# First layer's opening blocks in two halves of the features, with a new order of the opening

## The chip, the cores and the metric

The kernel runs on one core of a Trainium2 chip. The metric is the device time of one execution in microseconds (us); lower is better.

## The reference

A linear attention with a complex decay, then two layers of a feed-forward network; x has 3072 tokens of 384 columns.

```python
# attention: 4 batches, 8 heads, 768 steps, head width 48
mag = np.sqrt(a_re * a_re + a_im * a_im)
scale = np.minimum(mag, 0.999) / (mag + 1e-06)
for t in range(S):      # S = S * (a_re + i a_im) * scale + outer(k, v); y = q . Re(S)
    ...
# first layer, 384 -> 2048 -> 384
h = x @ w_in
x = (np.maximum(h, 0.0) + alpha * np.minimum(h, 0.0)) @ w_out
# second layer, 384 -> 2048 -> 384
h = x @ w_in2
out = (h - np.tanh(h)) @ w_out2
```

The weights come as 64-bit numbers.

## The kernel before

**The order.** The program is first recorded as operations, each with an engine, a length, what it reads and writes, and a rank ("want"). `Order.issue` then plays a list schedule: of the operations that could start earliest on an engine it takes the one of lowest rank. What it emits is a fixed order for each engine; the engines go through it in order and wait for each other by semaphores. All DMAs are issued from one queue, SP's, in order too: a DMA that waits holds up those behind it. The numbers at the end of the file (`UNITS`, `W_OFF`, `W_WANT`, `SEQ`, `PE_LO` and others) are ranks and choices that set this order.

**Attention.** The tokens are cut in 24 chunks of 128 and 12 units of two chunks; a batch has six chunks. `unit` loads `a_re` and `a_im`, takes squares, logarithms, exponentials and the angle on ACT and DVE, sums logarithms and angles over the steps with a triangular product on PE (L663), and makes `lc` (sum of logarithms, L669), `f` (reduced angle, L674 and L677) and `cs` (cosine and sine, L688 to L692). The cosine is taken from the magnitude of the angle, which L691 writes over `f`. The last row of `f` goes as `carry` to the next unit by a DMA (L682). `chunk` turns `k` and `q`, transposes them (L782), makes the scores (L792), the outputs (L810, L811) and the state (L822), and sends the result to DRAM (`x0d`, L842).

**Weights.** `weights` brings one of 16 features' groups of 128 (f = 0 to 15, "W0" to "W15"): two loads (L469, L467), an L479 on ACT, four integer steps on DVE (L35, L36, L37, L39), a high part on ACT (L487), and a low part: by DVE (L505), or for the f in `PE_LO` by PE and ACT: two halves of an L496 and an L497 product each, and two L499 copies.

**Layers.** `layer` takes blocks of 384 tokens (three chunks). A block's input is loaded as `xf`, split in a high (L865) and a low part (L868), together `xt`. For each f, `h` is a group of nine products (L882); ACT and DVE make `gg` (L889, L892), its high part `ghi` (L900) and low part `glo` (L902); a group of nine products adds them to three `acc` tiles (L913 in the first layer, L915 in the second). Behind f = 15 the three `acc` are copied and sent to DRAM (`x1d`), where the second layer fetches them. PSUM has two tiles for `h` and three for `acc`. `run` puts the eight blocks of the first layer one behind the other, 16 steps of rank each, and ranks the chunks by the block that needs them:

```python
for j in range(n0):
    self.layer(0, j, KF * j)
```

Block 0 needs chunks 0 to 2, which are units 0 and 1, and all 16 weights in its course; block 1 needs chunks 3 to 5.

Of the kernel before, what the change touches and what calls it, by code (L numbers as in the profile page):

```python
# [9 lines left out]
AF = mybir.ActivationFunctionType  # L10
# [342 lines left out]
class Fast:  # L353
# [167 lines left out]
    def unit(self, u, wants):  # L521
# [158 lines left out]
        if (u + 1) % self.UPB and u + 1 < self.NU:  # L680
            cy = ("carry", u + 1)
            self.D_(w0, 1536, lambda: nc.sync.dma_start(  # L682
                out=self.tile(cy, "carry", [1, HD]), in_=T[K("f", 1)][127:128, :]),
                r=[K("f", 1)], w=[cy], new=[(cy, "carry")])
        for c in range(2):
            f, cs = K("f", c), K("cs", c)
            f3 = lambda f=f: T[f].rearrange("p (h d) -> p h d", h=H)
            A(w0, HD, lambda cs=cs, f3=f3: nc.scalar.activation(  # L688
                out=self.tile(cs, "cs", [128, H, 2, D])[:, :, 1, :], in_=f3(), func=AF.Sin, scale=-TWO_PI),
              r=[f], w=[cs], new=[(cs, "cs")], tab=self.rank(u, "sin"))  # L690
            A(w0, HD, lambda f=f: nc.scalar.activation(out=T[f], in_=T[f], func=AF.Abs), w=[f])  # L691
# [32 lines left out]
    def chunk(self, u, j, w0):  # L724
# [23 lines left out]
        if not last:  # L748
            g = K("g")
            self.D_(w0, 1536, lambda: nc.sync.dma_start(out=self.gd[c:c + 1, :], in_=T[e][127:128, :]),  # L750
                    r=[e], w=[K("gd")])
# [5 lines left out]
            self.D_(w0, 1, gload, r=[K("gd")], w=[g], new=[(g, "g")])  # L757
# [90 lines left out]
    def layer(self, ph, j, step):  # L848
# [5 lines left out]
        for kt in range(KD):  # L854
# [17 lines left out]
        accs = [("acc", ph, j, i) for i in range(3)]  # L872
        for f in range(KF):
# [42 lines left out]
            P(step + f - 0.5, 9 * mm_us(n) if ph == 0 else 3 * n // 128 * mm_us(self.DM), g2, r=[gh, gl] + wp, w=accs,  # L916
              new=[(a, "acc") for a in accs] if f == 0 else ())
        for i in range(3):
            o = ("o", ph, j, i)
# [17 lines left out]
            self.D_(step + KF - 2000, 128 * n * 4, st, rate=300e3, r=[o], w=[("xd", 1, j, i)] if ph == 0 else [])  # L937

    def run(self):
# [26 lines left out]
        for j in range(n0):  # L966
            self.layer(0, j, KF * j)
# [74 lines left out]
SEQ = ['k1', 'r1', 'r0', 'a01', 'a00', 'r3', 'v1', 'q1', 'r5', 'r2', 'q0', 'a11', 'r6', 'a10', 'r4', 'k0', 'a21', 'a20', 'v0']  # L1042
# [4 lines left out]
KV_US = 0.85  # L1047
GENERAL = True
# [30 lines left out]
```

## Time and profile before

| | |
|---|---|
| time, median of 3 runs (lowest, highest) | 1079.32 us (1079.24, 1080.22) |
| the profiled execution: its time, its span | 1079.37 us, 1077.7 us |
| PE busy | 1015.8 us, 94% |
| DVE busy | 688.5 us, 64% |
| ACT busy | 612.3 us, 57% |
| moved by DMA | 73.72 MB |

Engines are PE (matrix products; PEld loads its weights), DVE (vector), ACT (scalar functions), POOL and SP (which issues the DMAs). A line such as L882 is the line of the kernel. "idle <-releaser" gives how long the engine stood before an instruction and what it then waited for. Busy shares are means over the span; the opening, in which attention and weights are made ready, has other limits than the rest.

### The profile page before, as it was taken

How to read it: one execution, taken by the hardware profiler on the slowest of the kernel's cores; microseconds unless marked ns; L12 is line 12 of the kernel's file. 1: busy time of each engine (PE TensorE's matmuls, PEld its weight loads, DVE VectorE, ACT ScalarE, POOL GpSimd, SP SyncE). 2: the span in 40 equal slices, each digit the busy share in tenths (PEclk: the TensorE clock that was granted, in tenths of full speed). 3: DMA queues.
4: the chain of work that ended last, by engine and by line, in shares of the span. 5: the costliest groups of instructions: out<-in, count | busy, mean ns of one | idle time of the engine just before them, and what ended most of it. 6: DMA issues, size and time to landing. Idle time of an engine off the chain costs nothing.

```text
span 1077.7 us, 17769 instructions
## 1 busy us (share of the span) xinstructions
PE 1015.8 (94%) x6872; PEld 975.0 (90%) x6872; DVE 688.5 (64%) x1219; ACT 612.3 (57%) x1226; POOL 2.8 (0%) x11
## 2 busy tenths in 40 slices
PE   1469999999999999999999999999999999999996
PEld 1257999999998999999999999999999999999996
DVE  6999987878478776488687489743333333433332
ACT  6987779857487775588574367443323332433331
POOL 1000000000000000000000000000000000000000
PEclk9699999999999999999999999999999999999998
DMA  9764162333223333131324224110101010100000
GB/s 269 188 159 111 31 168 53 74 75 78 59 49 67 60 75 80 46 68 30 75 55 152 89 96 162 59 44 1 44 1 45 1 45 1 45 8 23 16 8 26
DMA packets 184471, 73.72 MB, mean 68 GB/s; under 512 B 146469, under 2 KB 180281, under 8 KB 184377
## 3 DMA queue, kind: packets, MB, share of 16 engines
q1 hardware_dynamic: 184376, 72.49, 26.1%
q8 instruction: 56, 0.92, 0.4%
q14 instruction: 39, 0.31, 0.1%
HBM read 58.27 MB, written 14.19 MB: 67 GB/s over the span
## 4 chain that ended last, share of the span: by engine, by line
PE 81%; ACT 8%; DVE 5%; issue 2%; DMA 2%; SPq 1%; ACTq 0%; DVEq 0%
PE h L882 32%; PE acc L915 19%; PE acc L913 15%; PE x L782 4%; PE x L792 4%; PE x L810 2%; PE x L822 2%; PE x L811 2%; PE x L663 1%; DMA w<-in_moe_w_in_dram 1%; DVE glo L902 1%; ACT w L487 1%; SPq L543 1%; ACT ghi L900 1%; DVE gg L892 0%
## 5 line engine op out<-in xcount | busy, mean ns | idle before, releaser
L882 PE MATMUL h<-xt,w 128*128 128x384 f32 x2160 | 404.0, 337 | 5.2 <-DVE gg L892 4.1
L882 PEld LDWEIGHTS h<-xt,w 128*128 128x128 f32 x2160 | 375.7, 188 | 9.7 <-DVE gg L892 6.0
L902 DVE TENSOR_TENSOR glo<-gg,ghi 128x384 fp32r<-128x384 f32 x256 | 142.2, 556 | 99.0 <-ACT ghi L900 98.9
L900 ACT CAST ghi<-gg 128x384 fp32r<-128x384 f32 x256 | 131.2, 513 | 125.2 <-PE acc L915 42.6
L913 PE MATMUL acc<-ghi,w 128*128 128x384 f32 x768 | 199.9, 341 | 0.0
L915 PE MATMUL acc<-w,ghi 128*128 128x384 f32 x672 | 171.5, 336 | 1.8 <-ACT ghi L900 1.8
L898 DVE TENSOR_TENSOR gg<-h,gg 128x384 f32<-128x384 f32 x128 | 71.0, 554 | 157.8 <-ACT gg L896 157.8
L896 ACT ACTIVATE gg<-h 128x384 f32<-128x384 f32 x128 | 63.0, 492 | 163.9 <-PE h L882 159.5
L913 PEld LDWEIGHTS acc<-ghi,w 128*128 128x128 f32 x768 | 136.2, 188 | 3.5 <-issue 2.9
L913 PE MATMUL acc<-glo,w 128*128 128x384 f32 x384 | 129.1, 336 | 0.3 <-DVE glo L902 0.2
L915 PEld LDWEIGHTS acc<-w,ghi 128*128 128x128 f32 x672 | 121.9, 189 | 2.1 <-ACT ghi L900 2.1
L915 PE MATMUL acc<-w,glo 128*128 128x384 f32 x336 | 112.9, 336 | 0.0
L892 DVE SCALAR_TENSOR_TENSOR gg<-gg,nal,h 128x384 f32<-128x384 f32 x128 | 78.0, 610 | 47.2 <-ACT gg L889 46.7
L889 ACT ACTIVATE gg<-h 128x384 f32<-128x384 f32 x128 | 62.3, 487 | 56.2 <-PE h L882 54.5
L913 PEld LDWEIGHTS acc<-glo,w 128*128 128x128 f32 x384 | 72.1, 188 | 1.2 <-DVE glo L902 1.2
L915 PEld LDWEIGHTS acc<-w,glo 128*128 128x128 f32 x336 | 63.5, 189 | 0.2 <-DVE glo L902 0.2
L782 PE MATMUL x<-idt,kqt 128*112 128x128 f32 x384 | 55.2, 281 | 6.8 <-ACT w L499 6.4
L782 PEld LDWEIGHTS x<-idt,kqt 128*112 128x112 f32 x384 | 44.2, 137 | 12.4 <-ACT w L499 6.9
L792 PE MATMUL x<-qT,kT 112*128 112x128 f32 x384 | 51.2, 276 | 1.6 <-ACT kT L784 1.5
L792 PEld LDWEIGHTS x<-qT,kT 112*128 112x128 f32 x384 | 49.5, 192 | 3.5 <-ACT kT L784 2.6
L784 ACT COPY qT<-x 112x512 f32<-112x512 f32 x48 | 28.1, 586 | 34.9 <-PE x L782 32.5
L811 PE MATMUL x<-sc,v 128*48 128x128 f32 (+1 forms) x384 | 37.7, 274 | 0.0
(209 smaller groups left out, 1191.6 us busy)
## 6 DMA issues: line engine op xcount, KB each, us to landing
w<-in_moe_w_in_dram SPq DMA_DIRECT2D x16, 384.0 KB
w<-in_moe_w_out_dram SPq DMA_DIRECT2D x16, 384.0 KB
raw<-in_moe_w_in_dram SPq DMA_DIRECT2D x16, 384.0 KB
raw<-in_moe_w_out_dram SPq DMA_DIRECT2D x16, 384.0 KB
q<-in_q_dram SPq DMA_DIRECT2D x24, 192.0 KB
k<-in_k_dram SPq DMA_DIRECT2D x24, 192.0 KB
v<-in_v_dram SPq DMA_DIRECT2D x24, 192.0 KB
x0d<-sc SPq DMA_DIRECT2D x48, 96.0 KB
```

The lines of the kernel that those rows point to most:

```text
L782: nc.tensor.transpose(o[:, i, :], T[t][:, 4 * half + i], self.idt)
L792: nc.tensor.matmul(o[:, i, :], T[kT][:, i, :], T[qT][:, i, :], start=True, stop=True)
L811: nc.tensor.matmul(oh, cols(T[K("v")]), T[sc][:, i, :], start=first, stop=True)
L882: nc.tensor.matmul(o, w[:, a, kt * 128:(kt + 1) * 128], x[:, b_, kt, :n], start=i == 0, stop=i == len(mms) - 1)
L889: A(E, n, lambda h=h, g=g: nc.scalar.activation(out=mt(g, "gg"), in_=T[h][:, :n], func=AF.Relu, scale=-1.0), psum=True, r=[h], w=[g], new= ...
L892: V(E, n, lambda f=f, g=g, h=h: nc.vector.scalar_tensor_tensor(T[g][:, :n], in0=T[g][:, :n], scalar=self.nal[:, f:f + 1], in1=T[h][:, :n], ...
L896: A(E, n, lambda h=h, g=g: nc.scalar.activation(out=mt(g, "gg"), in_=T[h][:, :n], func=AF.Tanh), psum=True, r=[h], w=[g], new=[(g, "gg")], ...
L898: V(E, n, lambda h=h, g=g: nc.vector.tensor_tensor(T[g][:, :n], T[h][:, :n], T[g][:, :n], op=ALU.subtract), psum=True, r=[h], w=[g])
L900: A(E, n, lambda g=g, gh=gh: nc.scalar.copy(mt(gh, "ghi", F32R), T[g][:, :n]), r=[g], w=[gh], new=[(gh, "ghi")])
L902: V(E, n, lambda g=g, gh=gh, gl=gl: nc.vector.tensor_tensor(mt(gl, "glo", F32R), T[g][:, :n], T[gh][:, :n].bitcast(F32), op=ALU.subtract), ...
L913: nc.tensor.matmul(acc[:, :n], w[:, b_, i * 128:(i + 1) * 128], gs[a][:, :n], **kw)
L915: nc.tensor.matmul(acc, gs[a][:, i * 128:(i + 1) * 128], w[:, b_, :], **kw)
```

## The change

Each of blocks 0 and 1 is taken in two pieces of eight features. The order of the pieces is block 0 with f 0 to 7, block 1 with f 0 to 7, block 0 with f 8 to 15, block 1 with f 8 to 15, then blocks 2 to 7 whole. The first piece's sums are copied and sent to `x1d` in DRAM as before; the second piece loads them back into `xf` tiles (`part`), adds them to its `acc` on DVE and stores the result. For units 0 to 2 the magnitude of the angle goes to the place in `a` where the angle was, no longer over `f`. DMAs of `carry` and of the state's factor get a very low rank (`SOON`), so they are issued as soon as the planner has them ready. All ranks are new, and `PE_LO` has nine features, formerly five.

```diff
-            A(w0, HD, lambda f=f: nc.scalar.activation(out=T[f], in_=T[f], func=AF.Abs), w=[f])
...
+            m, key = f, [f]
+            if u < LATE:
+                m, key = ("turn", u, c), [arc[c]]
+            mag = lambda m=m, c=c: T[m] if m[0] == "f" else X("ai")[:, c * HD:(c + 1) * HD]
+            A(w0, HD, lambda f=f, mag=mag: nc.scalar.activation(out=mag(), in_=T[f], func=AF.Abs), r=[f] if u < LATE else [], w=key)
...
-    def layer(self, ph, j, step):
+    def layer(self, ph, j, step, f0=0, f1=None):
...
-        for kt in range(KD):
+        f1 = f1 or KF
+        for kt in range(KD) if f0 == 0 else ():
...
-        for f in range(KF):
+        for f in range(f0, f1):
...
+            if f0:
+                self.D_(done + 2000 - PART_AHEAD, 128 * n * 4, lambda i=i, part=part: nc.sync.dma_start(
+                    out=self.tile(part, "xf", [128, self.NB])[:, :n], in_=self.xd[1][i * 128:(i + 1) * 128, t0:t0 + n]),
+                    rate=300e3, r=[("xd", 1, j, i)], w=[part], new=[(part, "xf")])
...
+            if f0:
+                V(done, n, lambda i=i, o=o, part=part: nc.vector.tensor_tensor(
+                    self.tile(o, "sc", [128, self.NB])[:, :n], T[accs[i]][:, :n], T[part][:, :n], op=ALU.add),
+                  psum=True, r=[accs[i], part], w=[o], new=[(o, "sc")])
...
-            self.D_(w0, 1536, lambda: nc.sync.dma_start(
+            self.D_(w0 - SOON, 1536, lambda: nc.sync.dma_start(
...
-        for j in range(n0):
-            self.layer(0, j, KF * j)
+        for j, f0, f1 in PIECES:
+            self.layer(0, j, begin[j, f0], f0, f1)
...
+PIECES = [(0, 0, 8), (1, 0, 8), (0, 8, 16), (1, 8, 16)] + [(j, 0, 16) for j in range(2, 8)]
...
-PE_LO = (0, 3, 5, 7, 11)
+PE_LO = (1, 2, 3, 4, 5, 6, 8, 10, 11)
```

`UNITS`, `C_WANT`, `AHEAD`, `W_OFF`, `W_WANT`, `LATE_RANK` and `SEQ` get new values. In the changed file lines from 692 on stand 5 to 7 lower (L742 is L747, L882 is L889, L913 is L920). What the ranks do to the order is seen in three places.

SP's queue at the start, before (`w_112`, `w_117` are raw weights of W1 and W0, later ones of W3, W5, W2; `a` is unit 0's):

```order
L469 DMA w_112<-in_moe_w_in_dram 128x3x128
L467 DMA w_112<-in_moe_w_out_dram 128x384
L469 DMA w_117<-in_moe_w_in_dram 128x3x128
L467 DMA w_117<-in_moe_w_out_dram 128x384
L543 DMA a<-in_a_re_dram 128x8x48
L543 DMA a<-in_a_im_dram 128x8x48
```

and now, with the rows around the `carry` transfer further down (`w_123` and `w_132` are W0 and W1; `w_139` and `w_193` are the places of unit 1's and unit 2's `a`):

```order
L543 DMA a<-in_a_re_dram 128x8x48
L543 DMA a<-in_a_im_dram 128x8x48
L543 DMA a<-in_a_re_dram 128x8x48
L543 DMA a<-in_a_im_dram 128x8x48
L469 DMA w_123<-in_moe_w_in_dram 128x3x128
L467 DMA w_123<-in_moe_w_out_dram 128x384
...
L682 DMA carry<-f 1x16x24
L737 DMA q<-in_q_dram 128x8x48
L543 DMA w_139<-in_a_re_dram 128x8x48
L543 DMA w_139<-in_a_im_dram 128x8x48
L543 DMA w_193<-in_a_re_dram 128x8x48
L543 DMA w_193<-in_a_im_dram 128x8x48
```

The four loads of `a` moved ahead of the first weights, and the second halves of the next two units' `a` behind the `carry` of unit 0.

DVE ahead of the first `lc`, before (one piece of eleven rows; weight steps of W0 and W1 lie between the attention's):

```order
L35 TENSOR_SCALAR raw<-raw 128x768
L576 TENSOR_SCALAR hl<-a 128x384
L35 TENSOR_SCALAR raw<-raw 128x768
L36 TENSOR_SCALAR raw<-raw 128x768 x2
L579 SCALAR_TENSOR_TENSOR sq<-sq 128x384
L576 TENSOR_SCALAR hl<-a 128x384
L37 SCALAR_TENSOR_TENSOR raw<-w_112,raw 128x768
L37 SCALAR_TENSOR_TENSOR raw<-w_117,raw 128x768
L579 SCALAR_TENSOR_TENSOR sq<-sq 128x384
L39 SCALAR_TENSOR_TENSOR raw<-w_112,raw 128x768
L39 SCALAR_TENSOR_TENSOR raw<-w_117,raw 128x768
```

and now, where the weight steps begin with the first `lc`:

```order
L576 TENSOR_SCALAR hl<-a 128x384
L579 SCALAR_TENSOR_TENSOR sq<-sq 128x384
L576 TENSOR_SCALAR hl<-a 128x384
L579 SCALAR_TENSOR_TENSOR sq<-sq 128x384
L590 TENSOR_TENSOR hl<-hl,sq 128x384
L599 SCALAR_TENSOR_TENSOR sq<-sq,a 128x384
...
L669 TENSOR_SCALAR lc<-acc 128x384
L35 TENSOR_SCALAR raw<-raw 128x768 x2
L669 TENSOR_SCALAR lc<-acc 128x384
L36 TENSOR_SCALAR raw<-raw 128x768 x2
```

Eight weight steps moved from ahead of the first `lc` to behind it.

PE at the first `h` groups, before (`w0_177` is W0, `acc_987` the first of three sums):

```order
L882 MATMUL h_916<-xt_866,w0_177 128x384 x9
L882 MATMUL h_933<-xt_866,w1_173 128x384 x9
L882 MATMUL h_955<-xt_866,w2_253 128x384 x9
L882 MATMUL h_972<-xt_866,w3_264 128x384 x9
L913 MATMUL acc_987<-ghi_965,w0_177 128x384 x2
L913 MATMUL acc_987<-glo_970,w0_177 128x384
```

and now (`w10_967` is W10, whose low part PE makes):

```order
L889 MATMUL h_915<-xt_870,w0_214 128x384 x9
L889 MATMUL h_932<-xt_870,w1_203 128x384 x9
L889 MATMUL h_954<-xt_870,w2_282 128x384 x9
L920 MATMUL acc_975<-ghi_964,w0_214 128x384 x2
L920 MATMUL acc_975<-glo_969,w0_214 128x384
...
L496 MATMUL x_996<-raw_696,idt_72 128x384
L497 MATMUL x_996<-w10_967,hl_115 128x384
L496 MATMUL x_1004<-raw_696,idt_72 128x384
L497 MATMUL x_1004<-w10_967,hl_115 128x384
```

Three groups stand ahead of the first `acc`, and a pair for W10 stands behind it.

## Rows read from the trace of the kernel before

**Rows 1.** Page, part 1: busy time, share of the span, instructions of each engine.
```profile
PE 1015.8 (94%) x6872; PEld 975.0 (90%) x6872; DVE 688.5 (64%) x1219; ACT 612.3 (57%) x1226; POOL 2.8 (0%) x11
```

**Rows 2.** Stretches: length, busy us (count) of PE, PEld, DVE, ACT, POOL; PEclk, DMA share, GB/s.
```profile
27.00:54.00 27.00, 12.58 (x30) 6.19 (x30) 26.20 (x44) 25.48 (x46) 0.00 (x0) 0.62 0.80 188
54.00:81.00 27.00, 17.77 (x186) 13.91 (x186) 26.66 (x44) 23.18 (x42) 0.00 (x0) 0.94 0.59 157
81.00:108.00 27.00, 24.75 (x225) 19.61 (x223) 26.45 (x43) 20.72 (x42) 0.00 (x0) 0.93 0.45 111
108.00:135.00 27.00, 25.89 (x206) 24.87 (x207) 26.57 (x46) 20.04 (x37) 0.00 (x0) 1.00 0.17 31
...
162.00:189.00 27.00, 26.82 (x153) 25.75 (x151) 20.85 (x39) 25.12 (x54) 0.00 (x0) 1.00 0.24 55
189.00:216.00 27.00, 27.00 (x233) 25.89 (x233) 23.78 (x43) 23.14 (x47) 0.00 (x0) 1.00 0.37 72
```

**Rows 3.** Waits of PE after 110 us: total us, times, longest.
```profile
PE h L882 <- DVE gg L892: 2.5, 3, 1.1
PE acc L915 <- ACT ghi L900: 1.8, 1, 1.8
PE h L882 <- DVE gg L898: 0.8, 1, 0.8
```

**Rows 4.** Stretches between milestones, columns as in Rows 2.
```profile
22.58:104.87 82.29, 54.62 (x430) 38.69 (x428) 80.64 (x134) 70.25 (x132) 0.00 (x0) 0.83 0.63 154
112.34:180.70 68.36, 68.18 (x473) 65.54 (x472) 58.98 (x100) 53.88 (x104) 0.00 (x0) 1.00 0.39 98
```

**Rows 5.** Timeline of ACT: start us, us, engine, line, operation [idle before <-releaser].
```profile
7.94 1.28 ACT L479 ACT_TABLE_LOAD   x1 [7.94 <-DMA w<-in_moe_w_out_dram]
...
10.82 0.51 ACT L567 ACTIVATE sq<-a 128x384 f32<-128x384 f32 x1
```

**Rows 6.** Stretches of two microseconds, columns as in Rows 2.
```profile
2.00:4.00 2.00, 0.00 (x0) 0.00 (x0) 1.34 (x1) 0.00 (x0) 1.87 (x3) 1.00 0.90 273
4.00:6.00 2.00, 0.00 (x0) 0.00 (x0) 0.32 (x1) 0.00 (x0) 0.24 (x3) 1.00 0.99 326
6.00:8.00 2.00, 0.00 (x0) 0.00 (x0) 0.00 (x0) 0.06 (x1) 0.00 (x0) 1.00 1.10 313
8.00:10.00 2.00, 0.00 (x0) 0.00 (x0) 0.00 (x0) 1.99 (x2) 0.00 (x0) 1.00 1.12 215
```

**Rows 7.** Timeline of DVE: first lc, three after it, the third xt.
```profile
22.58 0.55 DVE L669 TENSOR_SCALAR lc<-acc 128x384 f32<-128x384 f32 x1
23.05 0.55 DVE L35 TENSOR_SCALAR w<-w 128x768 f32<-128x768 f32 x1
23.51 0.95 DVE L505 TENSOR_TENSOR w<-raw,w 128x768 fp32r<-128x768 f32 x1
24.38 0.55 DVE L36 TENSOR_SCALAR w<-w 128x768 int32<-128x768 int32 x1
...
104.33 0.54 DVE L868 TENSOR_TENSOR xt<-xf,xt 128x384 fp32r<-128x384 f32 x1
```

**Rows 8.** Timeline of PE: a weight-lo pair of two halves, and what follows it.
```profile
95.38 0.91 PE L496 MATMUL x<-w,idt 128*128 128x384 f32 x2
...
97.13 1.05 PE L792 MATMUL x<-qT,kT 112*128 112x128 f32 x8
```

**Rows 9.** Timeline of PE: first h groups, first acc group.
```profile
103.41 4.04 PE L882 MATMUL h<-xt,w 128*128 128x384 f32 x18
109.11 3.39 PE L882 MATMUL h<-xt,w 128*128 128x384 f32 x18 [1.66 <-DVE gg L892]
112.34 0.51 PE L913 MATMUL acc<-ghi,w 128*128 128x384 f32 x2
```

**Rows 10.** Waits of SP's own queue: total us, times, longest.
```profile
SPq L682 <- DVE f L677: 7.9, 2, 7.7
```

**Rows 11.** Chain of waits, in order of time: start us, us, what.
```profile
63.05 3.30 DMA x0d<-sc
```

More of the change, by code (lines that the diff above doesn't have):

```diff
@@ L871, in layer @@
         subs = [xt + (kt, i) for kt in range(KD) for i in range(2)]
-        accs = [("acc", ph, j, i) for i in range(3)]
-        for f in range(KF):
+        accs = [("acc", ph, j, f0, i) for i in range(3)]
+        for f in range(f0, f1):
             W = ("W", ph, f)
@@ L883, in g1 @@
                                      start=i == 0, stop=i == len(mms) - 1)
-            P(step + f, 9 * mm_us(n), g1, r=[xt] + subs + wp, w=[h], new=[(h, "h")])
+            P(step + f - f0, 9 * mm_us(n), g1, r=[xt] + subs + wp, w=[h], new=[(h, "h")])
             mt = lambda key, tag, dt=F32: self.tile(key, tag, [128, self.NB], dt)[:, :n]
-            E = step + f - 1000
+            E = step + f - f0 - 1000
             if ph == 0:
@@ L908, in g2 @@
                 for i in range(3):
-                    acc = self.tile(accs[i], "acc", [128, self.NB], psum=True) if f == 0 else T[accs[i]]
+                    acc = self.tile(accs[i], "acc", [128, self.NB], psum=True) if f == f0 else T[accs[i]]
                     for jj, (a, b_) in enumerate(((0, 0), (0, 1), (1, 0))):
-                        kw = dict(start=f == 0 and jj == 0, stop=f == KF - 1 and jj == 2)
+                        kw = dict(start=f == f0 and jj == 0, stop=f == f1 - 1 and jj == 2)
                         if ph == 0:
@@ L915, in g2 @@
                             nc.tensor.matmul(acc, gs[a][:, i * 128:(i + 1) * 128], w[:, b_, :], **kw)
-            P(step + f - 0.5, 9 * mm_us(n) if ph == 0 else 3 * n // 128 * mm_us(self.DM), g2, r=[gh, gl] + wp, w=accs,
-              new=[(a, "acc") for a in accs] if f == 0 else ())
+            P(step + f - f0 - 0.5, 9 * mm_us(n) if ph == 0 else 3 * n // 128 * mm_us(self.DM), g2, r=[gh, gl] + wp, w=accs,
+              new=[(a, "acc") for a in accs] if f == f0 else ())
+        done = step + f1 - f0 - 2000
         for i in range(3):
-            o = ("o", ph, j, i)
+            o, part = ("o", ph, j, f0, i), ("part", j, i)
+            if f0:
+                self.D_(done + 2000 - PART_AHEAD, 128 * n * 4, lambda i=i, part=part: nc.sync.dma_start(
+                    out=self.tile(part, "xf", [128, self.NB])[:, :n], in_=self.xd[1][i * 128:(i + 1) * 128, t0:t0 + n]),
+                    rate=300e3, r=[("xd", 1, j, i)], w=[part], new=[(part, "xf")])
             end = ph == 1 and j == len(self.blocks[1]) - 1
@@ L936, in st @@
                     nc.sync.dma_start(out=self.out[t0 + i * 128:t0 + (i + 1) * 128, :], in_=T[o])
-            self.D_(step + KF - 2000, 128 * n * 4, st, rate=300e3, r=[o], w=[("xd", 1, j, i)] if ph == 0 else [])
+            self.D_(done, 128 * n * 4, st, rate=300e3, r=[o], w=[("xd", 1, j, i)] if ph == 0 else [])
     def run(self):
@@ L959, in run @@
                 self.tile(neg, "hl", [128, 128], F32R), self.idt, -1.0, None, op0=ALU.mult), w=[neg], new=[(neg, "hl")])
+        begin, step = {}, 0
+        for j, f0, f1 in PIECES:
+            begin[j, f0] = step
+            step += f1 - f0
         for u in range(self.NU):
-            late = [KF * self.where[2 * u + c][0] - AHEAD + self.where[2 * u + c][1] / 256 + (c and C_WANT) for c in range(2)]
+            late = [begin[self.where[2 * u + c][0], 0] - AHEAD + self.where[2 * u + c][1] / 256 + (c and C_WANT) for c in range(2)]
             self.unit(u, UNITS[u] if u < len(UNITS) else [late[0], late[0], *late])
@@ L965, in run @@
             self.weights(0, f, W_WANT[0] + W_WANT[1] * f + (W_OFF[f]))
-        for j in range(n0):
-            self.layer(0, j, KF * j)
+        for j, f0, f1 in PIECES:
+            self.layer(0, j, begin[j, f0], f0, f1)
         for f in range(KF):
```

32 lines of the change are left out of this document (17 added, 15 removed).

## The prediction, made before the changed kernel was run

> **What bounds the kernel now.** I read the page first, then stretches of 27 us, then the waits of PE, then the three timelines around the first `h` product. The sum is made against the profiled execution, 1079.37 us (span 1077.7 us and 1.7 around it); the median of the three runs, 1079.32 us, is the same number for this purpose. A difference of about 0.2% (2.2 us) is what a measurement of this kernel can tell from none.
>
> The page says that PE is busy in 94% of the span [rows 1]. The reader should see in the stretches where the other 6% lie: PE worked 12.58, 17.77 and 24.75 us of the second to fourth stretch of 27 us, and nearly all of every later one [rows 2]. After 110 us it waited 5.1 us in all, in five waits [rows 3]. So the end is the moment at which PE can work without a break, plus the PE work left then, plus those few waits. Everything that the change can win lies in the first 112 us.
>
> In those, DVE is the limit: from its first `lc` to its third `xt` it was busy for 80.64 of 82.29 us, ACT for 70.25 [rows 4]. The timelines give the milestones: the first Square of the attention on ACT at 10.82 us, behind a table load and two weight steps that waited for weights until 7.94 [rows 5]; the first `lc` on DVE at 22.58; the third `xt` of block 0 at 104.33, the last input of an `h` group [rows 7]; the first `h` at 103.41 (a group's first products need less), with a wait of 1.66 us behind it, and the first `acc` product at 112.34 [rows 9].
>
> **The change, part by part.** Prices are starts of one instruction to starts of the next. On DVE 384 columns take 0.47 us (22.58 to 23.05), L35 and L36 with 768 columns 0.46, other work on 768 columns 0.87 (23.51 to 24.38) [rows 7].
>
> *A. Earlier head.* The four loads of `a_re` and `a_im` now stand first on SP, and ACT begins with a table load and the Square, no longer with weight steps. When do the loads land? Before, four weight loads (1.57 MB) stood first. 273, 326 and 313 GB/s in the slices from 2 to 8 us [rows 6] mean that they were through at about 7.2 us, and ACT started on the second pair at 7.94 [rows 5]: 0.75 us later. The pieces of `a` move more slowly; the slice from 8 to 10 us, in which they ran, has 215 GB/s [rows 6]. 197 KB at that rate are 0.9 us; from 2.3 us on that gives 3.2, with the 0.75 it is 4.0 us, and behind the table load of 1.28 us [rows 5] the Square starts at about 5.3. That is 5.5 us earlier. Ends: 6.2 earlier if the load runs at the full 326 GB/s and lands at once, 2.5 if the second pair holds the chain up. ACT and DVE have the same attention steps from there to the first `lc` as before, and the weight steps between them (5.4 us of DVE) only filled waits; so the whole head moves, and `lc` starts near 17.1.
>
> *B. DVE from the first `lc` to the third `xt`.* I count instructions in the two orders. The attention of chunks 0 to 3 stands ahead of the third `xt` in both. Now in this stretch: one L36, one L37 and two L39 more (0.47 + 0.87 + 1.74), and one L677 (0.47); gone are three L505 (2.61), one L576 and one L579 of the next unit (0.47 + 0.87), and two L614 of 768 columns (1.74). That is 2.1 us less of the 82.3. Its waits were 1.65 us before [rows 4]; I keep them. Ends: 1.7 us less, if nothing waits any more, and 4 more, if ACT now makes DVE wait: ACT has about as much work ahead of the third `xt` as before (three L479 and one L487 fewer; one Square, L674, L688, L696 and two L499 more) and had 12 us free in that stretch [rows 4]. Milestone: third `xt` at 104.3 - 5.5 - 2.1 = 96.7 us.
>
> *C. PE work left.* PE_LO has nine features for five, so 4 x 4 = 16 more instructions, L496 and L497. Two of the four additional features (W10 and W11) come behind the first `acc` product, where PE is the limit; the others lie in PE's idle time. A pair of halves took 97.13 - 95.38 = 1.75 us [rows 8], so +3.5 us. Ends 1.8 (half the price, if it pipelines better between full work) and 3.8. Four `h` groups stood ahead of the first `acc` product, now three: the first `acc` comes one group earlier and one group more is left, which cancels.
>
> *D. The halves themselves.* No product is added: block 0 and 1 have 8 + 8 features. Six stores and six loads of 192 KB are added, six adds on DVE (0.47) take the place of six copies on ACT, and six further copies on ACT save the partial sums. The partial of block 0 is stored when piece 1 ends and wanted when piece 3 ends, two pieces or some 50 us later; a round trip to DRAM starts with a store of the kind that took 3.30 us [rows 11]. The cover is that piece; without it each of the two blocks would cost about 6.6 us. SP sends these loads right after the stores, so what is late next would be `xf` loads behind them, and those of block 2 are wanted much later. Nothing. The magnitudes in `a` instead of `f` free `f` for the `carry` transfer; the same instruction, nothing.
>
> *E. Less slack behind the first product.* Before, the seventeenth `acc` group began at 180.70 us; from the first to it PE worked 68.18 of 68.36 us, DVE 58.98, ACT 53.88 [rows 4]. Between the same two groups the new order has more: on PE the two W-lo pairs (3.5 us) and some 1.5 us that come from further behind, together 73.3; on DVE nine instructions of 384 columns, four L35 or L36 and five others of 768 (4.2 + 1.9 + 4.4), together 69.5; on ACT 23 instructions, some 12 us. DVE would be busy for 95% and ACT for 90% of the time in which PE works without a break. The nearest stretches: with DVE at 98%, from 108 to 135 us, PE lost 1.1, most of it in the wait at 109; with ACT at 93%, from 162 to 189, it lost 0.18; with both at 86 to 88%, from 189 to 216, nothing [rows 2, 9]. Both near their limit at once does not occur. I take 0.5 us. Ends: 0 and 13 (below).
>
> Sum: -5.5 - 2.1 + 0 (halves) + 3.5 + 0.5 = -3.6 us; 1079.4 - 3.6 = **1075.8 us**.
>
> The granted clock was 0.62 from 27 to 54 us, a mix of its two levels (1.2 and 2.4 GHz) in a stretch in which PE had little to do; it was 0.94 and 0.93 in the two stretches before the first `h`, and 1.00, the upper level, after it [rows 2]. The Trainium skill, *TensorE: Matmul & The Clock Gate*, part 1, says that the array stands at half its rate after idling and returns once it has been busy; the rows agree. It speaks against a change that lets products start earlier behind a sparser start; by it the first groups would cost double, a rival below.
>
> **Rivals.**
> 1. *More is won.* The head moves by 6.2, DVE's waits in B vanish (-1.7), the W-lo pairs cost 1.8, E nothing: -6.2 - 2.1 - 1.7 + 1.8 = -8.2, 1071.2 us. For it: DVE has weight steps at hand wherever it waited. Against it: every term at its end.
> 2. *The start is lost on SP's queue, no difference.* The `carry` transfer now stands on SP ahead of `q`, the second halves of unit 1's and unit 2's `a`, W6 and more, and waits for `f` of unit 0; such a wait was 7.7 us before [rows 10], with only later loads behind it. DVE takes a clamp over both halves of unit 1 in order. If its data come 3 us late: -5.5 - 2.1 + 3 + 3.5 + 0.5 = -0.6, 1078.8 (1077 to 1081). Against it: by the milestones `f` is there near 28 us, the loads behind it land by 33 or 34, and the clamp is due at 33.
> 3. *The three engines starve each other, slower.* DVE can afford waits of 73.3 - 69.5 = 3.8 us in E for nothing; each further one moves the end. From 162 to 189 us it idled for 6.15 of 27 us [rows 2], mostly behind ACT. At that rate it would wait 16.7 us in E, 13 too many: 1079.4 - 4.1 + 13 = 1088; at two thirds of it 1083. It decides for slower where the waits pass 3.8 + 4.1 + 2.2 = 10.1 us. Against it: many of those waits came because PE was behind, not ahead.
> 4. *The clock.* Three `h` groups of 3.39 / 2 us [rows 9] at half rate cost 5.1 more: 1080.9. Against it: the attention products ahead of them are the same ones, and their stretch had 0.93.
>
> That the change does not do what it says can only mean that the first `h` waits for weights 8 to 15 anyway; in the new order none of its inputs is among them.
>
> **How the numbers follow.** Forecast 0.47 (its own range 1073.0 to 1078.2, of which 0.41 below 1077.2); rival 1 0.20; rival 2 0.17 (0.14 within 0.2%, 0.03 slower); rival 3 0.12; rival 4 0.04. Faster by over 0.2%: 0.41 + 0.20 = 0.61. Within: 0.06 + 0.14 = 0.20. Slower: 0.03 + 0.12 + 0.04 = 0.19. The range goes from 1070.5 to 1081.0: it takes in the forecast, rivals 1, 2 and 4, and leaves out rival 3 and a tail of rival 1, under 0.2 together.
>
> **What would show it.** Right: Square near 5.3 us, `lc` near 17, third `xt` near 97, first `acc` near 103, then at most 7 us of waits of PE. Step A is wrong if the Square starts after 7; step B if ACT is named in front of DVE for more than 4 us ahead of 97; C if a W-lo pair among `acc` groups takes less than 1.2 us; E if PE's stretches from 100 to 175 us lose more than 3 us. The forecast falls if the first `acc` comes after 106, or if PE waits for over 10 us behind it.

## The result, and the profile after

| | before | after |
|---|---|---|
| median (lowest to highest), 7 runs each | 1080.22 us (1079.15 to 1082.85) | 1086.93 us (1084.73 to 1088.84) |
| ratio, 95% interval | | 1.0057 (1.0043 to 1.007) |
| profiled execution: time, span | 1079.37, 1077.7 us | 1084.88, 1082.8 us |
| PE's first `acc` product | 112.34 us | 107.50 us |
| span behind it | 965.4 us | 975.3 us |

The change made the kernel slower by 0.6%; the forecast was 1075.8 us, in a range of 1070.5 to 1081.0. The first `acc` product came 4.84 us earlier, where the forecast's terms give 9.3 (to 103.0 us), and the rest of the program became 9.9 us longer, where they give 5.7 (3.5 for low parts, 1.7 for the `h` group that is left, 0.5 for waits).

Stretches of the kernel after, columns as in [rows 2]; the last two run from the first `lc` to the third `xt` and from the first `acc` product to the end:

```profile
27.00:54.00 27.00, 17.05 (x103) 11.67 (x101) 22.70 (x38) 24.59 (x47) 0.00 (x0) 0.75 0.83 194
54.00:81.00 27.00, 20.13 (x190) 15.38 (x192) 26.69 (x44) 24.73 (x44) 0.00 (x0) 1.00 0.69 182
81.00:108.00 27.00, 21.56 (x168) 16.65 (x166) 24.59 (x43) 21.08 (x43) 0.00 (x0) 0.94 0.37 96
...
243.00:270.00 27.00, 23.79 (x219) 21.64 (x218) 22.33 (x42) 17.13 (x36) 0.00 (x0) 1.00 0.61 137
...
16.24:101.28 85.04, 61.07 (x443) 42.71 (x442) 78.33 (x130) 72.44 (x136) 0.00 (x0) 0.90 0.69 176
...
107.50:1082.80 975.30, 958.10 (x6430) 931.78 (x6429) 595.31 (x1060) 526.40 (x1062) 0.00 (x0) 1.00 0.23 58
```

The same two of the kernel before that are not in [rows 2, 4]:

```profile
243.00:270.00 27.00, 27.00 (x212) 26.43 (x212) 22.81 (x43) 21.08 (x48) 0.00 (x0) 1.00 0.36 82
...
112.34:1077.70 965.36, 952.74 (x6409) 929.39 (x6408) 587.04 (x1046) 520.88 (x1056) 0.00 (x0) 1.00 0.22 56
```

DVE had 78.33 us of work from `lc` to `xt`, 2.3 less than in [rows 4], but the stretch is 2.75 us longer: its waits grew from 1.65 to 6.71 us. Behind the first `acc`, PE worked 5.36 us more (958.10 - 952.74) and waited 4.58 more (17.20 - 12.62). So the span is -4.84 + 5.36 + 4.58 = 5.1 us longer. The 5.36 are no surprise: the low parts of W10 and W11 took 3.27 us there, and one `h` group (1.7 us) more is left behind the first `acc`. PE's lost time between 243 and 270 us, 3.21 us, is new.

Timeline of ACT and DVE after: the table load, the Square, the first `lc`, DVE's three largest waits up to the third `xt`, and that `xt`:

```profile
0.82 1.28 ACT L567 ACT_TABLE_LOAD   x1 [0.82 <-PEq L1087]
...
3.67 0.52 ACT L567 ACTIVATE sq<-a 128x384 f32<-128x384 f32 x1 [1.57 <-DMA a<-in_a_re_dram]
...
16.24 0.55 DVE L669 TENSOR_SCALAR lc<-acc 128x384 f32<-128x384 f32 x1
...
29.50 0.56 DVE L35 TENSOR_SCALAR raw<-raw 128x768 f32<-128x768 f32 x1 [1.47 <-ACT raw L479]
...
47.02 1.25 DVE L669 TENSOR_SCALAR lc<-acc 128x384 f32<-128x384 f32 x2 [2.56 <-PE acc L663]
...
85.54 0.56 DVE L836 TENSOR_TENSOR s<-x,s 112x384 f32<-112x384 f32 x1 [1.60 <-PE x L827]
...
100.73 0.55 DVE L875 TENSOR_TENSOR xt<-xf,xt 128x384 fp32r<-128x384 f32 x1
```

Two of the three wait for PE, an engine that is busy for 63% of 27 to 54 us. Timeline of PE after:

```profile
41.61 1.93 PE L787 MATMUL x<-idt,kqt 128*112 128x128 f32 x8 [4.12 <-ACT w L499]
43.46 1.94 PE L827 MATMUL x<-v,kqt 128*64 128x48 f32 x32
45.34 2.34 PE L663 MATMUL acc<-w,tri 128*128 128x384 f32 x4
...
54.67 1.13 PE L827 MATMUL x<-v,kqt 128*64 128x48 f32 x32
...
58.66 1.04 PE L787 MATMUL x<-idt,kqt 128*112 128x128 f32 x8
...
94.98 1.65 PE L663 MATMUL x<-w,tri_t 128*128 128x384 f32 x2 [2.51 <-DVE w L623]
...
107.50 0.51 PE L920 MATMUL acc<-ghi,w 128*128 128x384 f32 x2
...
109.06 0.81 PE L496 MATMUL x<-raw,idt 128*128 128x384 f32 x2
...
110.69 0.51 PE L920 MATMUL acc<-ghi,w 128*128 128x384 f32 x2
```

The reader should compare equal instructions: after 4.12 us of idling L787 and L827 took 1.93 and 1.94 us, later 1.04 and 1.13. That is the lower clock level, and DVE waited for the L663 behind them. The stretch of these products shows it too (columns as in [rows 2]; the clock is the last but two):

```profile
41.60:47.60 6.00, 5.99 (x45) 4.69 (x46) 3.43 (x5) 4.21 (x9) 0.00 (x0) 0.55 0.96 256
```

The two halves of W10's low part took 1.63 us (109.06 to 110.69).

PE's waits from 107 us on (total us, times, longest), against [rows 3]:

```profile
PE x L787 <- DVE sc L799: 2.4, 1, 2.4
PE h L889 <- DVE gg L899: 2.0, 4, 0.8
PE acc L922 <- ACT ghi L907: 1.8, 1, 1.8
PE h L889 <- DVE gg L905: 1.4, 2, 0.9
PE x L797 <- ACT kT L789: 0.8, 1, 0.8
```

The first and the last of them stand at 256.8 and 263.2 us. All of PE's waits behind the first `acc` come to about 10 us; the other 7 of the 17.20 us stand behind its last product, before the change too.

### The profile page after: what moved, and what is told of

Its sections match the earlier page's. It is cut to its first block, busy times and chain, and to the rows that moved or that the text cites. A ratio compares the mean times of both kernels' runs of the same rounds, so it can differ in the third digit from the quotient of the medians.

```text
span 1082.8 us, 17838 instructions
## 1 busy us (share of the span) xinstructions
PE 1025.4 (95%) x6896; PEld 979.2 (90%) x6896; DVE 687.6 (63%) x1221; ACT 617.0 (57%) x1234; POOL 2.8 (0%) x11
## 4 chain that ended last, share of the span: by engine, by line
PE 80%; ACT 8%; DVE 6%; DMA 3%; issue 2%; SPq 1%; ACTq 0%; DVEq 0%
PE h L889 32%; PE acc L922 18%; PE acc L920 15%; PE x L797 4%; PE x L787 3%; DMA raw<-in_moe_w_out_dram 2%; PE x L815 2%; PE x L827 2%; PE x L663 2%; PE x L816 2%; PE acc L663 1%; DVE gg L899 1%; DVE glo L909 1%; ACT L710 1%; DMA w<-in_moe_w_out_dram 1%
## 5 line engine op out<-in xcount | busy, mean ns | idle before, releaser
L889 PE MATMUL h<-xt,w 128*128 128x384 f32 x2160 | 404.8, 337 | 5.5 <-DVE gg L899 4.0
L889 PEld LDWEIGHTS h<-xt,w 128*128 128x128 f32 x2160 | 375.3, 188 | 11.6 <-DVE gg L899 6.1
L920 PE MATMUL acc<-ghi,w 128*128 128x384 f32 x768 | 199.0, 340 | 0.2 <-ACT ghi L907 0.2
L920 PEld LDWEIGHTS acc<-ghi,w 128*128 128x128 f32 x768 | 136.6, 188 | 2.5 <-issue 1.5
L920 PE MATMUL acc<-glo,w 128*128 128x384 f32 x384 | 128.9, 336 | 0.8 <-DVE glo L909 0.8
L920 PEld LDWEIGHTS acc<-glo,w 128*128 128x128 f32 x384 | 72.1, 188 | 1.5 <-DVE glo L909 1.4
L787 PE MATMUL x<-idt,kqt 128*112 128x128 f32 x384 | 54.7, 277 | 9.8 <-ACT w L499 4.1
L787 PEld LDWEIGHTS x<-idt,kqt 128*112 128x112 f32 x384 | 44.0, 135 | 14.9 <-issue 9.1
L797 PE MATMUL x<-qT,kT 112*128 112x128 f32 x384 | 51.5, 277 | 4.0 <-ACT kT L789 2.2
L797 PEld LDWEIGHTS x<-qT,kT 112*128 112x128 f32 x384 | 48.9, 191 | 6.6 <-ACT kT L789 3.2
L799 DVE TENSOR_TENSOR sc<-x,tri 128x512 f32<-128x512 f32 x48 | 33.0, 687 | 15.1 <-PE x L797 9.8
```

The source lines that it names most:

```text
L787: nc.tensor.transpose(o[:, i, :], T[t][:, 4 * half + i], self.idt)
L797: nc.tensor.matmul(o[:, i, :], T[kT][:, i, :], T[qT][:, i, :], start=True, stop=True)
L799: V(w0 - 1, 512, lambda ps=ps, sc=sc: nc.vector.tensor_tensor(self.tile(sc, "sc", [128, 4, 128]), T[ps], self.mask.unsqueeze(1).to_broadca ...
L889: nc.tensor.matmul(o, w[:, a, kt * 128:(kt + 1) * 128], x[:, b_, kt, :n], start=i == 0, stop=i == len(mms) - 1)
```

## The experiments

Ratios are to the kernel before, run on the same chips. The clock is the mean granted clock of the single runs.

| kernel | median us | ratio (95% interval) | clock of the runs |
|---|---|---|---|
| after | 1086.93 | 1.0057 (1.0043 to 1.007) | 0.985 to 0.988 |
| 28 throwaway products, one place | 1085.94 | 1.0054 (1.0035 to 1.0073) | 0.985 to 0.995 |
| 173, five places | 1086.99 | 1.0063 (1.005 to 1.0076) | 0.995 to 0.997 |
| 15, one place | 1082.67 | 1.0026 (1.0015 to 1.0037) | 0.985 to 0.994 |
| 106 in eight places (96 in six took effect) | 1086.22 | 1.006 (1.0046 to 1.0074) | 0.987 to 0.993 |
| 134, nine places | 1080.32 | 0.9995 (0.9985 to 1.0006) | 0.992 to 0.999 |
| before, with 78 | 1079.15 | 0.9994 (0.9985 to 1.0003) | 0.993 to 0.999 |
| low parts of W10, W11 cut | 1083.70 | 1.0036 (1.0022 to 1.005) | 0.982 to 0.991 |
| blocks 0 and 1 whole | 1089.10 | 1.008 (1.0064 to 1.0095) | 0.982 to 0.989 |
| before's ranks, halves | 1102.22 | 1.0205 (1.0185 to 1.0226) | 0.974 to 0.979 |
| partial sums in `raw` | 1083.56 | 1.0023 (1.0014 to 1.0032) | 0.985 to 0.991 |
| 134 and partial sums in `raw` | **1077.12** | **0.9966 (0.9954 to 0.9979)** | 0.995 to 0.999 |

### Throwaway products where PE idled

A helper puts products of two constants ahead of a given group on PE, into a PSUM tile that nothing else uses at that time. The planner does not know of them, so every engine keeps its order.

```diff
-                    o = self.tile(ps, "x", [self.R, 4, 128], psum=True)
+                    o = self.warm(ps) or self.tile(ps, "x", [self.R, 4, 128], psum=True)
+WARM = {("xq", 0, 0, 0): 28}
+def warm(self, key):
+    if key in WARM:
+        d = self.ps.tile([128, self.NB], F32, tag="h", bufs=self.caps["h"], name="h")
+        for _ in range(WARM[key]):
+            self.nc.tensor.matmul(d[:, :128], self.idt, self.ones_t, start=True, stop=True)
```

> The changed kernel with the same order on every engine, and 28 throwaway products of 128 columns on PE ahead of the first product L787 of chunk 0, where PE stood idle for 4.12 us and then ran L787, L827 and L663 at half rate (1.93, 1.94 and 2.34 us, where later ones take 1.04, 1.13 and 1.56); DVE waited 2.56 us for that L663. Theory 1 (the opening's new waits of DVE are the array's low clock, and they set the end): these three run at full rate, the second lc comes near 44.7 us instead of 47.02, the first acc near 105.5 instead of 107.5, and the time falls by 1.5 to 2.4 us. Theory 2 (the queues' order sets the waits; what is won at 47 us is lost again at the wait of DVE for L827 at 85.5 us): second lc near 44.7, first acc within 0.5 us of 107.5, time within 0.5 us. Theory 3 (the work behind the first acc sets the end): first acc near 105.5, but PE waits up to 2 us more between 107 and 270 us, time within 0.7 us.

Timeline of PE in this run:

```profile
37.12 6.84 PE L1080 MATMUL h<-one,idt 128*128 128x128 f32 x56
43.80 1.04 PE L787 MATMUL x<-idt,kqt 128*112 128x128 f32 x8
44.76 1.13 PE L827 MATMUL x<-v,kqt 128*64 128x48 f32 x32
```

The products behind them ran at full rate, but one throwaway took 0.24 us, not the 0.13 that I had taken from L787; they held L787 up by 2.2 us (43.80 for 41.61) and ate what they won. Inconclusive (the first `acc` came at 108.25 us, 0.75 later, while the span was 0.2 us shorter), and so was the second kernel, with the same mistake at five places:

```diff
-WARM = {("xq", 0, 0, 0): 28}
+WARM = {("pl", 0, 0): 56, ("pt", 0, 0): 32, ("wl", 3, 0): 40, ("xq", 0, 0, 0): 28, ("pt", 2, 0): 17}
```

> As the run with 28 throwaway products, and more of them in four further idle stretches of PE: 56 ahead of the first L663 at 13.6 us, 32 ahead of the L663 at 21.2, 40 ahead of the L496 at 32.7, 17 ahead of the L663 at 95.0 us. All products that ran at half rate in the opening should run at full rate (granted clock 1.00 from 27 to 108 us instead of 0.75 and 0.94). Theory 1: DVE's wait of 1.47 us at 29.5 shrinks to under 0.7, the three L663 from 95.0 on take 2.1 us instead of 3.6, first acc near 104, time 3 to 5 us less, which takes back about all that the change lost. Theory 2: first acc not below 106.5, time at most 1 us less. Theory 3: first acc near 104, but the time only 0 to 1.5 us less, since PE's waits from 107 to 270 us grow by what was won.

Its first `acc` came at 112.14 us, 4.6 later than in the changed kernel, and its span was 3.5 longer. So a delay in the opening goes through to the rest: from 158 to 610 us the same instructions of this run stay 5.2 to 5.4 us later. That speaks against theory 3; whether a gain goes through as well, the 134 products below have to show. With the number set by the measured 0.24 us:

```diff
-WARM = {("xq", 0, 0, 0): 28}
+WARM = {("xq", 0, 0, 0): 15}
```

> The changed kernel with 15 throwaway products ahead of the first L787 of chunk 0, where 28 took 6.84 us (0.24 us each) and held that L787 up by 2.2 us. 15 take 3.6 of the 4.1 us in which PE stood idle. Theory 1 (half rate in the opening makes DVE's waits and they set the end): L787 near 41.6, at full rate, second lc near 45 instead of 47.0, first acc 1.5 to 2.4 us earlier, time 1.5 to 2.4 us less than that of the changed kernel. Theory 2 (order of the queues): first acc within 0.5 us of 107.5. Theory 3 (work behind the first acc) is out where the two runs before it moved the first acc by 0.7 and 4.6 us and the span followed.

The second `lc` came at 45.1 us as expected, DVE's wait there was gone, and the median is 0.3% below the changed kernel's (1.0026 to 1.0057). The profiled execution of this kernel (1086.1 us) does not show the gain: it fell to half rate elsewhere, near 76, 96 and 106 us, and DVE's wait for the L827 at 85 us grew from 1.6 to 2.9 us.

```diff
+WARM = {("pl", 0, 0): 34, ("pt", 0, 0): 16, ("wl", 3, 0): 18, ("xq", 0, 0, 0): 15,
+        ("xk", 1, 0, 0): 5, ("xs", 1, 0, 0): 6, ("xs", 1, 0, 1): 4, ("pt", 2, 0): 8}
```

> The changed kernel with 106 throwaway products in eight idle stretches of PE in the opening (34, 16, 18, 15, 5, 6, 4 and 8 of 0.23 to 0.27 us), each some 10 to 30 per cent shorter than the idle stretch. Theory 1: granted clock 1.00 from 27 to 108 us; DVE's waits in the opening fall from 6.7 to 3 to 4 us; first acc at 103 to 105 instead of 107.5; time 2.5 to 4.5 us less than the changed kernel's, and the runs spread less than its 1084.7 to 1088.8, whose slower ones had the lower clock. Theory 2: first acc above 106.5 and time within 1 us of the changed kernel's profiled 1084.9.

First `acc` at 104.63 us in the profile, but the median did not fall: a miss for theory 1 as I had put it. (Of the eight places two did nothing, since the products of the scores, L797, had no such call yet.) The profiled execution itself, 1084.01 us, is only 0.9 below the changed kernel's, though its first `acc` came 2.87 earlier: its third `h` group and first `acc` products ran at half rate (2.54 us for a group of 1.84), so that 2 us of the lead were left by 158 us, and from 648 to 702 us PE lost 2.65 us. The other runs had lower clocks than the profiled one, so more half rate; where, no profile shows. The next kernel gives the scores and the third `h` group their call too (the latter into an `acc` tile, free until then):

```diff
+WARM = {("pl", 0, 0): 36, ("pt", 0, 0): 18, ("wl", 3, 0): 28, ("xq", 0, 0, 0): 17, ("xk", 1, 0, 0): 7,
+        ("xs", 1, 0, 0): 7, ("xs", 1, 0, 1): 5, ("pt", 2, 0): 9, ("h", 0, 0, 2): 7}
```

> The changed kernel with 134 throwaway products in nine idle stretches of PE from 2.7 to 102 us. The run with 106 of them still had half rate at 31.5 to 34.9 us and at 103.2 to 106.6 us, where PE had idled 2.6 and 1.8 us; these two are filled now (28 instead of 18 there, 7 ahead of the third h group), and so are 71.7, 76.0 and 79.4 us, where other runs fell to half rate. If half rate in the opening is what makes this kernel's runs differ (1084.7 to 1088.8): granted clock 1.00 from 8 us to the end of the work, first acc near 103.5 instead of 104.6, runs within 2 us of each other, and the median 1081 to 1083, 4 to 6 us below the changed kernel's. If something else makes them differ, the median stays at 1085 to 1087 with a full clock. By the account of work and waits behind the first acc (975 us in the changed kernel, 965 in the one before) it cannot come below 1080.

Stretches, with the one from the first `lc` to the third `xt` first:

```profile
16.35:97.54 81.19, 74.41 (x625) 59.71 (x624) 78.22 (x130) 72.18 (x136) 0.00 (x0) 0.98 0.73 187
27.00:54.00 27.00, 24.70 (x224) 20.12 (x223) 26.05 (x44) 26.81 (x50) 0.00 (x0) 1.00 0.98 236
...
81.00:108.00 27.00, 25.49 (x191) 20.92 (x187) 25.44 (x45) 23.65 (x48) 0.00 (x0) 1.00 0.33 82
```

Timeline of PE:

```profile
40.74 1.06 PE L787 MATMUL x<-idt,kqt 128*112 128x128 f32 x8 [0.82 <-ACT w L499]
41.72 1.13 PE L827 MATMUL x<-v,kqt 128*64 128x48 f32 x32
42.78 1.56 PE L663 MATMUL acc<-w,tri 128*128 128x384 f32 x4
...
103.61 0.51 PE L920 MATMUL acc<-ghi,w 128*128 128x384 f32 x2
```

The granted clock is 0.98 from the first `lc` to the third `xt` and 1.00 in the two others, DVE's waits fell from 6.71 to 2.97 us (81.19 - 78.22) with the same work, the first `acc` came at 103.61 us, and the median lies 0.6% below the changed kernel's and no longer differs from the kernel before. So by the medians half rate in the opening cost the changed kernel about as much as it lost. The two traces show part of this: of the 5.8 us between the profiled executions 3.8 to 3.9 were won by the first `acc`, and the same instructions keep this lead up to 610 us. The other 1.9 come between 610 and 680 us, at the second layer's start, and are not shown to come from the clock. DVE's wait of 1.6 us for the L827 at 85 us stayed as it was. The control asks whether any kernel here gains that:

```diff
 # in the kernel before; "mid" stands between the two products of a low part
+WARM = {("pt", 0, 0): 13, (("wl", 3, 0), "mid"): 8, ("wl", 5, 0): 21, (("wl", 5, 0), "mid"): 12, ("xk", 1, 0, 0): 24}
```

> The control: the kernel before, in its own order, with 78 throwaway products where its PE ran at half rate in the opening (13 ahead of the L663 at 28.4, 8 between the products at 34.9, 21 ahead of the L496 at 43.1, 12 between the products at 48.3, 24 ahead of the L782 at 80.5 us). Its DVE waited for only 1.65 us from the first lc to the third xt, so by theory 1 the clock costs it little: first acc 111 to 112.3 (112.34 before), time 0 to 1.2 us less. If the low clock costs every kernel of this kind the same, it gains as much as the changed kernel does, 2.5 us or more.

First `acc` at 111.43 us, and no difference in time that can be measured, though the clock of the kernel before had been lower still (0.980 to 0.986). What half rate costs depends on who waits for the products.

### The low parts of W10 and W11

```diff
-                    nc.tensor.matmul(t, self.idt, T[cv].bitcast(F32)[:, sl], start=True, stop=False)
-                    nc.tensor.matmul(t, T[neg], part(0)[:, sl], start=False, stop=True)
+                    f in (10, 11) or nc.tensor.matmul(t, self.idt, T[cv].bitcast(F32)[:, sl], start=True, stop=False)
+                    nc.tensor.matmul(t, T[neg], part(0)[:, sl], start=f in (10, 11), stop=True)
```

> The changed kernel in the same order, but the low parts of W10 and W11 are left incomplete: of each half only the L497 product is made, L496 is left out (four L496 of about 0.45 us at full work). Tells what the two pairs among the acc groups cost. If PE sets the end there (step C): PE works 1.8 us less and the time falls by 1.5 to 2.0 us. If DVE and ACT set it (the pairs stand in PE's slack): the time falls by less than 0.5 us and PE's waits up to 270 us grow by as much.

Timeline of PE: both L497 of W10 and what follows them, a wait, and the seventeenth `acc` group.

```profile
109.79 0.51 PE L497 MATMUL x<-w,hl 128*128 128x384 f32 x2
110.13 0.51 PE L920 MATMUL acc<-ghi,w 128*128 128x384 f32 x2
...
112.38 0.65 PE L787 MATMUL x<-idt,kqt 128*112 128x128 f32 x4 [0.53 <-DVE kqt L772]
...
182.30 0.60 PE L920 MATMUL acc<-ghi,w 128*128 128x384 f32 x2
```

The stretches from the first to the seventeenth `acc` group, in the changed kernel and in this one:

```profile
107.50:181.87 74.37, 73.22 (x495) 69.02 (x494) 70.42 (x122) 62.43 (x123) 0.00 (x0) 1.00 0.44 109
108.23:182.30 74.07, 71.93 (x486) 67.32 (x486) 70.42 (x122) 62.46 (x123) 0.00 (x0) 1.00 0.44 110
```

W10's pair took 0.34 us instead of 1.63 and W11's 0.97 (0.20 of it a wait) instead of 1.64, so about 2 us less for two, but the stretch became only 0.3 us shorter: PE waited instead, first for DVE. The ratio fell by 0.0021, 2.3 us, but the two intervals meet, and five of the nine runs had a clock of 0.991, above any of the changed kernel (0.985 to 0.988). So the median does not show that the pairs lie on the path, and the trace speaks for the expectation's other case: DVE, busy for 70.42 us in both, needs nearly as long as PE here.

### Halves alone, and ranks alone

```diff
-PIECES = [(0, 0, 8), (1, 0, 8), (0, 8, 16), (1, 8, 16)] + [(j, 0, 16) for j in range(2, 8)]
+PIECES = [(j, 0, 16) for j in range(8)]
```

> The changed kernel with all its new ranks, but blocks 0 and 1 whole, not in halves: no partial sums. The opening up to the first acc keeps its order; behind it W8 to W15 are wanted by block 0 at once. Theory a (the halves cost little themselves and give DVE time for W8 to W15): PE then waits 4 to 8 us between 135 and 162 us, the waits near 257 us go or shrink, time 1 to 5 us more. Theory b (the halves are what costs, by their copies, adds, round trips and the early demand for block 1's attention): waits behind the first acc fall from 10 to about 5 us and the time falls by 3 to 5 us.

1089.1 us: slower than the changed kernel by 0.2%, where the intervals still meet. PE lost 2.4 us from 135 to 162 us and 2.6 from 162 to 189, and nothing from 243 to 270. Theory b is out, since nothing was won without the halves; theory a's 4 to 8 us of waits came, but spread over twice the stretch. The reverse:

```diff
 # the changed file with the kernel before's UNITS, C_WANT, AHEAD, W_OFF, W_WANT, LATE_RANK, PE_LO, SEQ
-SOON = 3105.8
+SOON = 0
-            if u < LATE:
+            if False:
                 m, key = ("turn", u, c), [arc[c]]
```

> One part alone: the kernel before with its own ranks and PE_LO, but blocks 0 and 1 in halves (no magnitudes in a's place, no low rank for the small DMAs). The order up to the first acc is that of the kernel before. If halves by themselves relieve DVE behind the first acc, PE waits there no longer than the 3.7 us of before and the time is 1077 to 1081. If halves want block 1's attention eight groups earlier than these ranks make it (chunks 3 to 5 for group 8 instead of 16), PE waits 10 to 20 us between 130 and 165 us and the time is 1088 to 1100.

PE's waits in this run, the longest group:

```profile
PE h L889 <- ACT xt L872: 10.8, 3, 6.7
```

Group 8 is now block 1's first, and its input was not there. The time, 1102.22 us, is above the range that was expected. The halves need the new ranks; the ranks without the halves are no faster than both together. So neither part by itself wins anything.

### The place of the partial sums

In the changed kernel all of block 2's input came late. Its SP queue:

```profile
253.33 0.42 SPq L929 DMA_DIRECT2D xf<-x1d  x1
255.21 0.53 SPq L950 DMA_DIRECT2D x1d<-sc  x1
255.79 0.42 SPq L865 DMA_DIRECT2D xf<-x0d  x1
...
261.31 0.93 SPq L865 DMA_DIRECT2D xf<-x0d  x2
```

`xf` has two buffers, and the partial sums (L929) are loaded into them. Block 2's inputs (L865 in the changed file) are issued as the adds (L938, at 252.35, 254.63 and 258.90 us) let go of the buffers, and from 251.7 to 267 us PE has only attention products.

```diff
-                    out=self.tile(part, "xf", [128, self.NB])[:, :n], in_=self.xd[1][i * 128:(i + 1) * 128, t0:t0 + n]),
-                    rate=300e3, r=[("xd", 1, j, i)], w=[part], new=[(part, "xf")])
+                    out=self.tile(part, "raw", [128, self.NB])[:, :n], in_=self.xd[1][i * 128:(i + 1) * 128, t0:t0 + n]),
+                    rate=300e3, r=[("xd", 1, j, i)], w=[part], new=[(part, "raw")])
```

> The changed kernel, but the partial sums that come back from DRAM are loaded to a buffer of raw instead of to one of the two xf buffers. Theory P (the partial sums hold both xf buffers: block 2's inputs could only be loaded at 255.8 and 261.3 us, when the adds L938 had let go of them, so PE had only attention products from 248 to 267 us and waited 3.2 us): block 2's xf loads go out before the end of the fourth piece, PE's waits from 243 to 270 us fall from 3.2 to under 0.5, the waits behind the first acc from 17.2 to about 14 (8.8 of them at the very end), time 2.5 to 3.5 us less than the changed kernel's. Theory R (block 2's attention is late by its ranks, and PE would wait for it anyway): the waits there stay over 2 us, time within 1 us. The opening and its half rate stay as they are.

All three L865 were issued together at 236.25 us, PE lost nothing from 243 to 270 us, the idle time behind the first `acc` fell to 14.7 us, and the ratio to 1.0023. The profiled execution (1085.08 us) does not show the gain: it had more half rate in the opening, and its first `acc` came at 109.94 us. Both changes in one kernel:

> Both: the 134 throwaway products and the partial sums in raw. If the two losses are separate they add: first acc near 103.6 as with the 134 products alone, PE's waits from 243 to 270 us under 0.5, time 2.5 to 3.5 us below the 1080.3 of that run, 1076.8 to 1077.8, which is below the kernel before and near the 1075.8 that was predicted for the change. If PE's wait at 257 us only moves on (the second layer's weights from 648 us, or block 3's attention), time 1079 to 1081.

SP's queue, and the stretch that had lost 3.21 us:

```profile
229.31 7.32 SPq L865 DMA_DIRECT2D xf<-x0d  x3
```

```profile
243.00:270.00 27.00, 27.00 (x169) 26.87 (x167) 18.95 (x35) 13.95 (x29) 0.00 (x0) 1.00 0.51 132
```

1077.12 us: the two losses add, and this version is below both kernels. Against the profiled execution with the 134 products alone the span is 2.2 us shorter (1077.0 to 1074.8); of the 3.2 us of PE that is what came through.

## Why the prediction was wrong

**A, the head: right, and more than forecast.** The Square started at 3.67 us (5.3 forecast) and `lc` at 16.24 (17.1). Most of this is the table load: I had put its 1.28 us behind the data, but it ran from 0.82 to 2.10 us, while they were still on their way. The data were there at 3.67, only 0.3 before the 4.0 that I had taken.

**B, DVE's work: right; "Its waits were 1.65 us before [rows 4]; I keep them": the step that failed.** The work fell by 2.31 us (2.1 forecast), the waits rose by 5.06. I had asked whether ACT had time to spare; ACT is named for 1.8 us. For 4.4 us DVE waited for PE, which had more time to spare than any other but ran at half rate. With the clock held up 3.74 of the 5.06 us went; the other 1.3, most of it the wait for the L827 at 85 us, stayed, and no run tells what it comes from. The forecast third `xt`, 96.7 us, then came at 97.04 us, and the first `acc` (103 forecast) at 103.61; that it came so near is in part luck, since these 1.3 us and the 0.7 us that the head was earlier than forecast nearly cancel.

**The clock, rival 4: the right mechanism in the wrong place.** I priced it at the three `h` groups alone and ruled out the attention products, "the same ones", because their stretch had 0.93 before. But 0.93 was the stretch from 81 us on; from 27 to 54 us it was 0.62 [rows 2], and there the change moved them. Before, PE had low parts of weights in that stretch, and the first L782 came only at 50.82 us. It took 1.93 us too, but the L663 came right behind it:

```profile
50.82 1.93 PE L782 MATMUL x<-idt,kqt 128*112 128x128 f32 x8 [0.18 <-DVE kqt L767]
52.53 1.52 PE L663 MATMUL acc<-w,tri 128*128 128x384 f32 x2
...
54.10 0.56 DVE L669 TENSOR_SCALAR lc<-acc 128x384 f32<-128x384 f32 x1 [0.28 <-PE acc L663]
```

DVE had other steps until 53.8 us and waited for 0.28, and none of its waits from there to the third `xt` was over 0.3. After, that product stands at 41.61 us, L827 with its 1.94 us stands between it and the L663, DVE's order has only an L35 at 43.05 us and an L592 at 43.52 left before the second `lc`, and DVE waited 2.56 us.

**C, low parts: the price right, the place not shown.** 1.63 and 1.64 us for 1.75 each. That PE alone is the limit there does not hold: with some 2 us less of them the stretch became 0.3 us shorter.

**D, halves: wrong by one buffer.** Copies, adds and the round trip cost nothing that a wait names. But "those of block 2 are wanted much later" looked at SP's queue and not at the buffers: two of `xf`, both taken by partial sums. It cost 3.2 us of PE, which went when the partial sums were put elsewhere. This is the second step that failed: the term stood at nothing.

**E, the slack: right where it was placed.** From the first to the seventeenth `acc` group PE lost 1.15 of 74.37 us, against 0.18 of 68.36 before; 73.8 were forecast. By the sign as worded, 100 to 175 us, it lost 3.10, just over the 3 that were to show E wrong; but 1.96 of that stand ahead of the third `h` group, where the kernel before had waited 1.66. Of the other new waits, 1.5 us more lie from 648 to 702 us, at the second layer's weights. PE lost 0.86 to 2.65 us in that stretch in five further runs of this same order, so I don't put them to the change.

**Sum.** Forecast -3.6; measured on the profiles +5.5 us in time (+5.1 in span). Both signs that the forecast falls were there: the first `acc` after 106 us, and about 10 us of waits of PE behind it. The throwaway products bring the ratio down by 0.0062 (6.7 us), the partial sums' place by 0.0034 (3.7), both by 0.0091 (9.8): what is left, 1077.1 us, is near the 1075.8 whose sum had left these two out, and by its ratio 3.7 us below the kernel before, where 3.6 were forecast. Rival 3 came nearest with its price (1083 to 1088), but by luck: its place, the first seventeen `acc` groups, lost little.

## What to carry to other kernels

When a change brings work forward, look at what the engine that must do it was doing just before: on PE, products behind an idle stretch took up to twice their time here (1.93 us for 1.04), and the busy share of that engine tells nothing of it. Compare equal instructions in both traces. Filling such a gap with products that nobody reads is cheap if their length is first measured and they end before the real data come. Ask first who waits for the slow products: the kernel before had a lower clock and gained nothing from it.

For each new tile, count the buffers of its tag and who else draws from it in the same stretch; a queue with room is no cover.

## What the runs showed of the hardware

- The length of an idle stretch does not by itself tell the rate behind it: before, a pair of L663 products took 0.91 us at 28.43 after 3.75 us of idling; after, an equal pair took 1.65 us at 94.98 after 2.51 us.
- One order of instructions gives different times: the changed kernel's seven runs go from 1084.73 us (clock 0.988) to 1088.84 (0.986), the mended one's from 1076.54 (0.999) to 1079.35 (0.995). The Trainium skill, *TensorE: Matmul & The Clock Gate*, part 1, says that the number of products at half rate changes from run to run of a kernel; these clocks agree. So one profile can understate such a loss: the changed kernel's own, 1084.88 us, is 4 us below its slowest run.
- A throwaway product of 128 columns in f32 shows the level at once: in the kernel with 134 it took 0.43 us from start to start at the lower level (17.3 to 19.4 us) and 0.22 at the upper (from 19.8 us). The averages of 0.23 to 0.27 us by which their number was set mix the two.
- The granted clock of a stretch is no witness for the first 27 us of the changed kernel. It reads 1.00 from 20 to 27 us, though the pair of L663 there took 1.65 us, where an equal pair took 0.91 at 55.73 us (a stretch, columns as in [rows 2], and a line of PE's timeline):

```profile
20.00:27.00 7.00, 5.78 (x11) 3.24 (x11) 7.00 (x12) 5.93 (x12) 0.00 (x0) 1.00 0.96 244
...
21.22 1.65 PE L663 MATMUL acc<-a,tri_t 128*128 128x384 f32 x2 [3.66 <-ACT a L610]
```
